# Splitting the stores of the last two heads of an attention backward pass unevenly over the DMA engines

## The chip, the core and the metric

One core of a Trainium2 chip runs the kernel. The metric is device time in microseconds; the median of eight runs of the kernel before is 1289.58 us. The core has five compute engines (TensorE = PE, VectorE = DVE, ScalarE = ACT, GpSimd = POOL, SyncE = SP) and 16 DMA engines that move data between memory and the on-chip buffer of 128 partitions. GpSimd and SyncE issue the DMAs; each has a queue of its own on every DMA engine (in the profile q0 is GpSimd's, "software_dynamic", and q1 SyncE's, "hardware_dynamic").

## The reference

Softmax attention with one query per head, forward and backward, for 2 x 32 = 64 heads, 8192 keys and a head size of 128, all in bfloat16:

```python
def _fwd_reference(q, k, v):
    scale = q.shape[-1] ** -0.5
    scores = jnp.einsum("bhqd,bhkd->bhqk", q, k) * scale
    p = _softmax(scores, axis=-1)
    return jnp.einsum("bhqk,bhkd->bhqd", p, v)

def reference(q, k, v, grad_out):
    out, vjp = jax.vjp(_fwd_reference, q, k, v)
    return (out, *vjp(grad_out))          # out, dq, dk, dv
```

k and v are 2 MB per head, and so are dk and dv. dk of a head is an outer product of a vector over the keys and the query, dv one of the probabilities and grad_out. The kernel reads and writes 268 MB each.

## The kernel before

Heads are numbered 0 to 63. Each head has two tiles, k (w = 0) and v (w = 1), of 128 partitions x 64 keys x 128 values; a partition's row is 16 KB and contiguous in memory. Twelve such tiles fit (`NTILE`), so loads run six heads ahead of the work (`AHEAD`). A tile is loaded (`load`, L98, SyncE), transposed on TensorE (L184), copied by ScalarE (L186), used for scores and for the two accumulations (L195, L339), and at last overwritten in place by `outer` (L394, VectorE) with dk or dv, from where it is stored.

One loop over g, eight steps per head, holds everything in a hand-written order; each instruction is pinned. `outer(i, w, c, ends)` makes quarter c of dv (steps 9 to 12 of a head) or dk (steps 13 to 16), and when c + 1 stands in `ends` it issues the store of what is ready. For all heads but the last `ends` is `whole` = [4], one store of 2 MB per tensor. For the last head it is `last` = [1, 2, 3, 4], one store of 512 KB for each quarter.

Who stores: dk and dv of heads 0 to 62 go by GpSimd (`store_eng`), L412. The last head's eight quarters go by SyncE (`load_eng`), L412 too, then the two small stores of dq and out (L489). dk of the heads 5, 14, ... 59 (`SPREAD`) goes in two pieces, 126 rows and 2 rows, through `by_rows` (L87), which issues one DMA for each number of rows that it is given:

```python
    def by_rows(eng, dst, src, rows):
        p = 0
        for m in rows:
            pin(eng.dma_start(out=dst[p : p + m], in_=src[p : p + m], max_dma_last_dim=NT * D))
            p += m
```

At the start of the kernel the cursor of GpSimd's DMAs is reset (L108, `inc_swdge_sem(..., mode="reset_dge_cursor")`), and GpSimd loads 6 rows of q while SyncE loads the other 58.

A tile's next load waits until the store from it has landed. The framework has eight semaphores for GpSimd's DMAs and eight for SyncE's and uses each in turn: a GpSimd store also waits until the GpSimd store eight before it has landed, and a SyncE DMA until the SyncE DMA eight before it has. At the end of the program SyncE waits for every DMA (L515).

Of the kernel before, what the change touches and what calls it, by code (L numbers as in the profile page):

```python
# [20 lines left out]
SPREAD = range(5, 64, 9)  # L21
# [3 lines left out]
def kernel(  # L25
# [16 lines left out]
    BH = B * H  # L42
# [3 lines left out]
    NCH = NT // CH  # L46
# [3 lines left out]
    load_eng = nc.sync  # L50
    store_eng = nc.gpsimd
    pin = tc.keep_in_program_order
# [30 lines left out]
# [6 lines that stand above are left out]
# [299 lines left out]
    def outer(i, w, c, ends):  # L388

        h = heads[i]  # L390
        n0 = c * CH
        shape = [P, CH, D // 2, 2]
        pin(
            nc.vector.tensor_tensor(  # L394
                out=h.tile[w][:, n0 : n0 + CH, :].rearrange("p n (e t) -> p n e t", t=2),
                in0=h.qb[w][:]
                .rearrange("p (e t) -> p e t", t=2)
                .unsqueeze(1)
                .to_broadcast(shape),
                in1=h.pair[w][:, n0 : n0 + CH, :].unsqueeze(2).to_broadcast(shape),  # L400
                op=ALU.mult,
            )
        )
        if c + 1 in ends:
            at = ends.index(c + 1)
            b0, b1 = (ends[at - 1] if at else 0) * CH, (c + 1) * CH
            dst = (dv_v if w else dk_v)[i]
            if w == 0 and i in SPREAD:
                by_rows(store_eng, dst, h.tile[w], (P - 2, 2))
            else:  # L410
                eng = load_eng if len(ends) > 1 else store_eng
                pin(eng.dma_start(out=dst[:, b0:b1, :], in_=h.tile[w][:, b0:b1, :]))  # L412
# [3 lines left out]
    A0 = A1 + NCH  # L416
    O0 = A0 + 1
    whole = [NCH]
    last = list(range(1, NCH + 1))
    AHEAD = NTILE // 2  # L420

    prev = None
    for g in range(SL * BH + O0 + NCH + 4 - SL):
# [15 lines left out]
        if x := within(O1):  # L439
            outer(x[0], 1, x[1], last if x[0] == BH - 1 else whole)  # L440
        if x := within(O0):
            outer(x[0], 0, x[1], last if x[0] == BH - 1 else whole)
        ev = None
        if g < SL * BH:
            i, r = divmod(g, SL)
# [74 lines left out]
```

## Time and profile before

| | |
|---|---|
| median of 8 runs | 1289.58 us (1285.62 to 1291.8) |
| profiled execution: its own time | 1290.0 us |
| profiled execution: span | 1288.2 us |
| PE / DVE / ACT / POOL busy | 88% / 73% / 76% / 6% |
| HBM read, written | 268.47 MB, 268.47 MB; 417 GB/s over the span |
| last store by GpSimd (dk of head 62) issued | 1245.02 us |
| stores of the last head by SyncE issued | 1247.44 to 1258.1 us |
| small stores of dq and out issued | 1260.86 and 1265.1 us |

The span is the time from the first to the last instruction; the profiled execution's own time is 1.8 us longer. In the profile all times are in us from the start of the span. L12 is line 12 of the kernel. A DMA that a queue issues lands when its last byte is confirmed; between the two lies the time in the queues of the 16 DMA engines. A slice or stretch has a DMA share: the mean share of time in which the 16 engines were busy, so 0.5 can be eight engines at work and eight at rest.

### The profile page before, as it was taken

The numbers are of one execution on the slowest core, as the hardware profiler recorded it, in microseconds if no ns is written. First come the engines' busy times: TensorE is split into PE (matmuls) and PEld (weight loads), VectorE is DVE, ScalarE is ACT, GpSimd is POOL, SyncE is SP. The second block draws the span as 40 slices with busy tenths as digits, with TensorE's granted clock in tenths as the row PEclk, the third lists the DMA queues.
The fourth block names the chain that finished last, engine by engine and source line by source line (L and its number), as shares of the span: only waits on it lengthen the run. The fifth ranks groups of instructions, "written<-read, shape, count | busy, mean of one in ns | idle before, by whom it ended". The sixth has DMA issues, their size and how long they took to land.

```text
span 1288.2 us, 42575 instructions
## 1 busy us (share of the span) xinstructions
PE 1133.8 (88%) x19268; PEld 861.2 (67%) x19268; DVE 936.2 (73%) x2122; ACT 975.7 (76%) x641; POOL 75.3 (6%) x142
## 2 busy tenths in 40 slices
PE   6999999988998988989889898899888988988880
PEld 5777777766676666766667676667666766766650
DVE  2888888777687777767677786778677777777681
ACT  6888888877787777877777787778677777777750
POOL 0000000000000000000000000000000000000000
PEclk9999999999999999989899899999999999999885
DMA  9999999999999999999999999999999999999995
GB/s 387 424 428 428 425 427 428 428 427 427 427 427 426 427 427 427 413 428 427 427 427 426 426 426 427 428 427 424 426 428 428 426 425 423 428 428 427 426 389 208
DMA packets 39986, 539.68 MB, mean 419 GB/s; under 512 B 5116, under 2 KB 5116, under 8 KB 6396
## 3 DMA queue, kind: packets, MB, share of 16 engines
q1 hardware_dynamic: 20172, 272.70, 49.8%
q0 software_dynamic: 19632, 264.25, 48.7%
q8 instruction: 150, 2.46, 0.7%
q14 instruction: 32, 0.26, 0.0%
HBM read 268.47 MB, written 268.47 MB: 417 GB/s over the span
## 4 chain that ended last, share of the span: by engine, by line
DMA 45%; PE 20%; another core or an unknown queue 18%; DVE 10%; issue 3%; ACT 1%; SPq 1%; POOL 0%; DVEq 0%; POOLq 0%; ACTq 0%
DMA kvt<-in_v_dram 24%; DMA kvt<-in_k_dram 17%; PE tp L184 9%; DVE kvt L394 6%; PE acc L339 5%; DMA out_dram<-kvt 3%; PE sw L195 2%; PE dpw L195 2%; DVE sel L362 2%; ACT ev L186 1%; DVE sel L356 1%; SPq L98 1%; PE dpw L282 1%; DMA qd_nat<-in_q_dram 1%
## 5 line engine op out<-in xcount | busy, mean ns | idle before, releaser
L186 ACT COPY ev<-tp 128x2048 bf16<-128x2048 bf16 x512 | 954.9, 1866 | 267.3 <-PE tp L184 256.2
L184 PE MATMUL tp<-ident_bf,kvt 128*128 128x128 bf16 x8192 | 560.9, 223 | 92.2 <-DMA kvt<-in_v_dram 73.8
L394 DVE TENSOR_TENSOR kvt<-qb,pair 128x2048 bf16<-128x2048 bf16 x512 | 621.3, 1214 | 0.4
L184 PEld LDWEIGHTS <-kvt 128*128 128x128 bf16 x8192 | 491.4, 101 | 99.1 <-DMA kvt<-in_v_dram 77.5
L195 PEld LDWEIGHTS <-ev 128*128 128x128 bf16 x8192 | 243.0, 96 | 209.3 <-issue 152.8
L339 PE MATMUL acc<-kvt,dS_pad 128*64 128x512 bf16 x1024 | 169.2, 413 | 0.8 <-DVE dqT L379 0.8
L339 PE MATMUL acc<-kvt,E_pad 128*64 128x512 bf16 x1024 | 161.1, 395 | 0.0
L195 PE MATMUL dpw<-qdT,ev 128*128 128x1 bf16 x4096 | 140.7, 164 | 16.6 <-DVE qb L177 15.8
L362 DVE SCALAR_TENSOR_TENSOR sel<-acc,diag,sel 128x128 f32<-128x128 f32 x384 | 134.7, 351 | 13.6
L195 PE MATMUL sw<-qdT,ev 128*128 128x1 bf16 x4096 | 141.9, 164 | 1.1 <-ACT ev L186 1.1
L412 POOL DMA_DIRECT2D out_dram<-kvt x119 | 64.0, 537 | 1091.6 <-DVE kvt L394 896.4
L207 DVE TENSOR_REDUCE mp<-sw 128x1 f32<-128x64 f32 x64 | 14.4, 225 | 155.6 <-PE sw L195 155.6
L339 PEld LDWEIGHTS <-dS_pad 128*64 128x64 bf16 x1024 | 37.7, 111 | 24.9 <-issue 6.1
L247 DVE CAST E_pad<-E_f 128x64 bf16<-128x64 f32 x64 | 12.5, 195 | 56.4 <-ACT E_f L238 56.4
L339 PEld LDWEIGHTS <-E_pad 128*64 128x64 bf16 x1024 | 36.5, 109 | 21.4 <-issue 0.9
L376 PE MATMUL acc<-ones,sel 128*128 128x1 f32 x256 | 43.5, 239 | 6.2 <-DVE sel L362 6.2
L282 PE MATMUL dpw<-ld,ones 128*128 128x1 f32 x256 | 46.3, 250 | 0.1
L253 DVE CUSTOM_DVE_ANT_0 junk<-E_f,dpw 128x64 bf16<-128x64 f32 x64 | 14.2, 221 | 41.9 <-PE dpw L195 41.9
L376 PEld LDWEIGHTS acc<-ones,sel 128*128 128x128 f32 x256 | 39.3, 194 | 7.3 <-DVE sel L362 7.3
L356 DVE TENSOR_SCALAR sel<-acc,diag 128x128 f32<-128x128 f32 x128 | 44.1, 345 | 0.0
L177 DVE CAST qb<-dpw 128x128 bf16<-128x128 f32 x128 | 35.5, 277 | 6.0 <-PE dpw L168 6.0
L282 PEld LDWEIGHTS dpw<-ld,ones 128*128 128x128 f32 x256 | 38.2, 188 | 0.5 <-DVE ld L253 0.5
(44 smaller groups left out, 313.2 us busy)
## 6 DMA issues: line engine op xcount, KB each, us to landing
out_dram<-kvt POOLq DMA_DIRECT2D x119, 2048.0 KB, 67.2
kvt<-in_v_dram SPq DMA_DIRECT2D x64, 2048.0 KB, 20.7
kvt<-in_k_dram SPq DMA_DIRECT2D x63, 2048.0 KB, 20.7
out_dram<-kvt POOLq DMA_DIRECT2D x7, 2016.0 KB, 70.8
out_dram<-kvt SPq DMA_DIRECT2D x8, 512.0 KB, 24.5
kvt<-in_k_dram SPq DMA_DIRECT2D x2, 512.0 KB, 4.6
kvt<-in_k_dram SPq DMA_DIRECT2D x1, 1024.0 KB, 7.2
out_dram<-kvt POOLq DMA_DIRECT2D x7, 32.0 KB, 70.5
```

The lines of the kernel that those rows point to most:

```text
L177: pin(nc.vector.tensor_copy(out=h.qb[w][:], in_=h.qbp))
L184: pin(nc.tensor.transpose(tp[:, t, :], src[:, c * CH + t, :], ident_bf[:]))
L186: pin(nc.scalar.copy(out=ev[:], in_=tp[:]))
L195: nc.tensor.matmul(dst[:, c * CH + t : c * CH + t + 1], lhsT=ev[:, t, :], rhs=qdT[:, w, i : i + 1], start=True, stop=True,)
L207: pin(nc.vector.reduce_max(out=h.mp[:], in_=h.s, axis=AX.X))
L282: nc.tensor.matmul(out, lhsT=ones[:].to_broadcast([P, P]), rhs=col, start=True, stop=True)
L339: nc.tensor.matmul(h.acc[w][g : g + CW, :], lhsT=wts[:, n0 : n0 + CW], rhs=rows[:, n0 : n0 + QT, :].rearrange("p n d -> p (n d)"), start=( ...
L356: nc.vector.tensor_scalar(out=h.sel[:], in0=block, scalar1=diag[:, 0:1], scalar2=None, op0=ALU.mult)
L362: nc.vector.scalar_tensor_tensor(out=h.sel[:], in0=block, scalar=diag[:, b : b + 1], in1=h.sel[:], op0=ALU.mult, op1=ALU.add,)
L376: nc.tensor.matmul(h.acc[w][:, 0:1], lhsT=h.sel[:], rhs=ones[:], start=True, stop=True)
L394: nc.vector.tensor_tensor(out=h.tile[w][:, n0 : n0 + CH, :].rearrange("p n (e t) -> p n e t", t=2), in0=h.qb[w][:] .rearrange("p (e t) -> ...
L412: pin(eng.dma_start(out=dst[:, b0:b1, :], in_=h.tile[w][:, b0:b1, :]))
```

## The change

The stores of head 62 and the cut of head 63's stores change. dv of head 62 is stored by GpSimd in three pieces of 15, 95 and 18 rows, after a reset of GpSimd's DMA cursor. dk of head 62 goes by SyncE, not GpSimd, in three pieces of 76, 48 and 4 rows. The last head's stores are issued in halves (two for dv, two for dk) where they were issued in quarters. By the author's words the piece of 95 rows lies on DMA engines 15 and 0 to 3.

```diff
@@ outer
             dst = (dv_v if w else dk_v)[i]
-            if w == 0 and i in SPREAD:
+            if i == BH - 2 and w == 1:
+                pin(store_eng.inc_swdge_sem([], [], mode="reset_dge_cursor"))
+                by_rows(store_eng, dst, h.tile[w], (15, 95, 18))
+            elif i == BH - 2:
+                by_rows(load_eng, dst, h.tile[w], (76, 48, 4))
+            elif w == 0 and i in SPREAD:
                 by_rows(store_eng, dst, h.tile[w], (P - 2, 2))
@@ before the loop
     whole = [NCH]
-    last = list(range(1, NCH + 1))
+    last = [NCH // 2, NCH]
     AHEAD = NTILE // 2
```

In the order of the built program nothing else moves. GpSimd's queue ends with the reset and the pieces of 15, 95 and 18 rows in place of two whole stores. SyncE's ends with the pieces of 76, 48 and 4 rows, four halves and the two small stores; the second small store shares its semaphore with the piece of 76 rows and so waits for that piece to land. The changed kernel's lines behind the change are five higher (L412 is L417, L515 is L520).

## The prediction

> **What bounds the kernel now.** I read the page's slices first. They show what is scarce.
>
> ```profile
> DMA  9999999999999999999999999999999999999995
> GB/s 387 424 428 428 425 427 428 428 427 427 427 427 426 427 427 427 413 428 427 427 427 426 426 426 427 428 427 424 426 428 428 426 425 423 428 428 427 426 389 208
> ```
>
> The 16 DMA engines are busy in every slice but the last, at some 427 GB/s. That is 26.7 GB/s an engine, so a row of one head (one partition, 16 KB) costs an engine 0.61 us. The changed stores move the same bytes, so only the last slice (1256 to 1288 us) can give or take anything. Second, the table of stretches of 2 us over the end; the columns that matter are the last two, DMA share and GB/s.
>
> ```profile
> 1258.00:1260.00 2.00, 0.58 (x2) 0.50 (x2) 1.22 (x5) 0.00 (x0) 0.00 (x0) 0.50 1.03 418
> ...
> 1262.00:1264.00 2.00, 0.00 (x0) 0.00 (x0) 0.00 (x0) 0.00 (x0) 0.00 (x0) 0.50 0.67 278
> 1264.00:1266.00 2.00, 0.00 (x0) 0.00 (x0) 0.00 (x0) 0.00 (x0) 0.00 (x0) 0.50 0.57 240
> ...
> 1270.00:1272.00 2.00, 0.00 (x0) 0.00 (x0) 0.00 (x0) 0.00 (x0) 0.00 (x0) 0.50 0.53 222
> ...
> 1278.00:1280.00 2.00, 0.00 (x0) 0.00 (x0) 0.00 (x0) 0.00 (x0) 0.00 (x0) 0.50 0.41 171
> 1280.00:1282.00 2.00, 0.00 (x0) 0.00 (x0) 0.00 (x0) 0.00 (x0) 0.00 (x0) 0.50 0.21 82
> ...
> 1284.00:1286.00 2.00, 0.00 (x0) 0.00 (x0) 0.00 (x0) 0.00 (x0) 0.00 (x0) 0.50 0.12 47
> ```
>
> Times 16, the share counts engines at work: all until 1260, 9 at 1265, 8 at 1271, 7 at 1279, 3 at 1281, 2 at 1285. No compute engine works after 1262. The end is therefore a queue on a few engines while the rest are done. Third, SyncE's waits and the DMA issues say the same from the other side.
>
> ```profile
> SPq L515 <- DMA out_dram<-kvt: 20.5, 4, 17.1
> ```
> ```profile
> out_dram<-kvt POOLq DMA_DIRECT2D x119, 2048.0 KB, 67.2
> kvt<-in_v_dram SPq DMA_DIRECT2D x64, 2048.0 KB, 20.7
> out_dram<-kvt SPq DMA_DIRECT2D x8, 512.0 KB, 24.5
> ```
>
> SyncE's last act is to wait 17.1 us for dk of head 62. A GpSimd store takes 67 us to land, a load 21 us: the wait is in the store queues of the slowest engines.
>
> The packet records have no engine number, but a packet of a busy engine starts 4 ns before its forerunner ends, so I chained them to 16 engines. Their last packets of 4 KB or more end at 1261.4 to 1263.9 (seven engines), 1272.0, 1272.7, 1278.6, 1280.4, 1280.5, 1280.8, 1281.7, 1285.8 and 1286.1, as the shares say. The cause shows too: the 150 instruction packets (16 KB, about 0.98 us) rotate over the same eight engines, 18 or 19 each, some 18 us an engine. Seven of these eight are the seven that end last.
>
> **Which engines get which rows.** In the records the six-row load took six engines, the 58-row load of q by SyncE two engines (29 packets each), a 126-row store fourteen engines (nine rows each) and the two-row piece the other two, the same two in all seven heads. I read this as: the count of engines is the largest number up to 16 that divides the rows, and GpSimd's pieces go round from a cursor. After a reset, then: 15 rows, one each on engines 0 to 14; 95 rows, 19 each on 15 and 0 to 3; 18 rows, two each on 4 to 12. SyncE: 76 rows, 19 each on four engines; 48, three each on all; four, one each on four. No row shows that SyncE's four are 0 to 3; I take it. Of head 62 an engine had 16 rows. It now has 43 (0 to 3), 6 (4 to 12), 4 (13, 14) or 22 (15).
>
> [...]
>
> **Part by part.**
> - Ten rows less on a late engine: 10 x 0.61 = 6.1 us. 1286.0 becomes 1279.9, and the group at 1278.6 to 1281.7 becomes 1272.5 to 1275.6. This lies on the path that sets the end.
> - 27 rows more on engines 0 to 3: 16.5 us. If all four are of the seven early ones, 1262 becomes 1278.5, up to 1280.4 for the latest of the seven. It hides behind the 1279.9 by a hair.
> - Six rows more on engine 15: 3.7 us, 1266 or, if it is one of the two near 1272, 1276. Hidden.
> - The pieces' waits. Each GpSimd store waits for the landing of the GpSimd store eight before it. dv of 62 went at 1234.73: its data was ready at 1234.44, and dk of 58 had landed at 1165.16 + 68.4 = 1233.6. The 15 rows go then too; the 95 rows wait for dv of 59 (issued 1174.24, 64.2 us to land: 1238.4); the 18 rows wait for dk of 59 (1185.36 + 61.8 = 1247.2). Behind them GpSimd has nothing. Engines 0 to 3 must start the 19 rows before they run dry; with 1.1 to 1.6 us from a GpSimd issue to its first packet (the records of dk and dv of 62) that is 1240, and 19 + 23 + 16 rows are then 35 us of work: 1275 plus what is still queued. If the 95 rows came as late as 1247.3, stepping those engines forward row by row gives 1282, a gain of 4 instead of 6.
> - The reset of the cursor: 18 ns at the one place where it stands now (L108). Three issues of 0.58 to 0.80 us (L87's) for one of 0.53: under 2 us of GpSimd, which idles. Nothing, unless the 95 rows are the bound.
> - dk of 62 on SyncE: ready at 1244.7 as now. Three issues stand ahead of dv of 63. The eight stores there cost 0.34 to 1.39 us each, so 4.2 us at most: 1249.2, and the first half of dv of 63 is ready at 1249.4. No cost. If it were 3 us more, the late engines would still have store rows until past 1264.
> - Halves for quarters: per engine 32 packets of 8 KB for 64 of 4 KB, the same 9.8 us. The first two quarters leave 2 us later, the last half at the time of the last quarter (1258.1); on an idle engine it ends 1.2 us later, 1263. Hidden behind 1280 on every engine; 1.2 us if that cover were gone.
> - The second small store of out_0 waits now for the 76 rows' landing: 76 packets of 8 KB in turn on two queues from 1246, 23 us, 1269. The store then needs a few us (the queue makes up its 21.6 now). Hidden by 11 us.
>
> Sum: the last packet goes from 1286.0 to 1279.9 with engines 0 to 3 beside it; from there to the end of the span it was 2.2 us and stays so. The span becomes 1282.2. The profiled execution took 1290.0 with a span of 1288.2, so 1284.0; the median of the eight runs is 1289.58, 0.4 below the profiled one, which I leave inside the range.
>
> **The rivals.**
> - Slower: the heavy share falls on an engine that is not early. It decides from an engine that ended after 1286.0 - 16.5 = 1269.5, and nine of sixteen did. Against it: the relieved pair is 4 and 5 if the cursor stood at 6 after the six-row load, and of this pair one fetches instructions and one does not (it has 511 stretched packets instead, 53 us, and ends at 1272.7). Were the eight fetchers neighbours, they would be 5 to 12, and 0 to 3 early. In my chains the two engines of the 58-row load (0 and 1) end early too, though chains can have swapped. For it: the engine that ends at 1272.0 neither fetches nor is relieved; it is one of 2, 3, 13, 14 and 15, two in five for the heavy ones. Then 1272.0 + 16.5 = 1288.5, the time 1292.5; with a fetching engine among 0 to 3, 1295 to 1302.6, the time 1299 to 1307. [...]
> - Late pieces: the 95 rows held back until 1247 by the semaphore or by room in the queue, 1286 to 1287. For it, GpSimd's stores took up to 74.6 us to land, and 74.6 after 1174.24 is 1248.8; against it, the landing that counts took 64.2 here.
> - The change doesn't do what it says: the pieces spread evenly or over other engines. Late engines save 0 to 4 us: 1286 to 1290.
>
> **How the numbers follow.** About 0.2% (2.6 us) can be told from no change. Forecast 0.52 (1282 to 1286, point 1284.0); late pieces 0.10; spread evenly 0.12, of which most within 0.2%; heavy engine not early 0.26, of which 0.22 slower by over 0.2% and 0.04 within. That makes faster 0.63, same 0.15, slower 0.22. The forecast's own range is 1281.5 to 1286.5; the range reaches into the slower case at its lower price, 1293.5, and leaves out the fetching engine and a little below.
>
> **What would show it.** Right: the share after 1264 stays near 0.7 (0 to 3 and the seven late ones) and falls steeply at 1276 to 1280; dv of 60 to dk of 61 land as before; the GpSimd store of 95 rows is issued near 1238.4, the 18 rows near 1247; SyncE's last wait ends near 1280. Wrong: a share of 0.06 to 0.25 beyond 1283 (one to four engines with the heavy share), or a late issue of the 95 rows, or a late group that ends at 1286 as now.

## The result and the profile after

The changed kernel takes 1302.49 us (median of 11 runs, 1296.14 to 1311.95), the kernel before beside it 1288.52 us (32 runs): ratio 1.0109, interval 1.0093 to 1.0125. It is slower by 1.1%, some 14 us. The prediction of 1284.0 and its range up to 1293.5 both missed. The profiled execution took 1299.66 us, less than the median; its span is 1297.9 us.

The page's slices of the changed kernel first: the share of the DMA engines, and what they moved.

```profile
DMA  9999999999999999999999999999999999999994
GB/s 390 424 427 426 427 427 427 426 428 429 426 427 428 426 427 423 425 427 425 429 428 426 427 428 427 428 424 425 425 428 428 426 426 424 428 427 429 423 315 145
```

Up to slice 38 (1233 us) nothing differs. In slice 39 (1233 to 1265 us) the engines are as busy as ever (a 9), but move 315 GB/s; slice 39 of before, 1224 to 1256 us, had 389. The table of stretches over the same stage says it more sharply; the last two columns are the DMA share and GB/s. The kernel before:

```profile
1236.00:1262.00 26.00, 16.68 (x173) 9.82 (x170) 22.06 (x48) 6.72 (x6) 0.53 (x1) 0.69 0.96 384
1262.00:1280.00 18.00, 0.00 (x0) 0.00 (x0) 0.00 (x0) 0.00 (x0) 0.00 (x0) 0.50 0.52 218
```

The changed kernel:

```profile
1236.00:1262.00 26.00, 14.91 (x142) 8.58 (x137) 20.39 (x43) 5.04 (x5) 1.62 (x2) 0.66 0.94 314
1262.00:1280.00 18.00, 0.00 (x0) 0.00 (x0) 0.00 (x0) 0.00 (x0) 0.00 (x0) 0.50 0.73 245
...
1284.00:1286.00 2.00, 0.00 (x0) 0.00 (x0) 0.00 (x0) 0.00 (x0) 0.00 (x0) 0.50 0.25 103
...
1288.00:1290.00 2.00, 0.00 (x0) 0.00 (x0) 0.00 (x0) 0.00 (x0) 0.00 (x0) 0.50 0.18 72
1290.00:1292.00 2.00, 0.00 (x0) 0.00 (x0) 0.00 (x0) 0.00 (x0) 0.00 (x0) 0.50 0.06 25
```

Divide GB/s by the share and you have what all 16 engines would move if none rested: before 384 / 0.96 = 400 and 218 / 0.52 = 419, after 314 / 0.94 = 334 and 245 / 0.73 = 336. A busy engine moves a sixth to a fifth less. The share alone, which the prediction counted engines by, doesn't show it. In the packet records of 1245 to 1275 us a 16 KB packet takes 732 ns on average (619 before) and one of 8 KB 410 ns (316 in 300 to 1200 us). Most packets keep their time, the medians are 611 and 309 ns; about a quarter take over a tenth longer, these 1.07 us and 0.68 us on average. Summed over all packets behind 1232 us, the time beyond 611, 309 and 159 ns for 16, 8 and 4 KB is 130 us of engine time; before it was 22. I call this sum the stretch. It is one thing that went wrong. The other is at the end of the table: four engines at work at 1285 (0.25 x 16), three at 1289, one from 1290 to 1296.

Which engines these are can be read from the packet records, though they have no engine number: a packet of a busy engine starts some 4 ns before its forerunner ends, so the last ones can be followed back. SyncE's piece of four rows is two packets of 8 KB and one of 4 bytes on each of its four engines alone. The chains that end at 1283.6, 1289.2, 1289.9 (here one record is missing) and 1296.1 us have these packets directly ahead of their 32 packets of halves. So the three engines that end last are three of those with 43 rows.

The issues lie where the prediction had them. GpSimd's timeline, with the idle time before each instruction and its releaser:

```profile
1225.48 0.53 POOL L417 DMA_DIRECT2D out_dram<-kvt  x1 [11.67 <-DVE kvt L394]
1233.13 0.60 POOL L87 DMA_DIRECT2D out_dram<-kvt  x1 [7.12 <-DVE kvt L394]
1236.27 1.03 POOL L87 DMA_DIRECT2D out_dram<-kvt  x1 [2.54 <-DMA out_dram<-kvt]
1243.47 0.59 POOL L87 DMA_DIRECT2D out_dram<-kvt  x1 [6.17 <-DMA out_dram<-kvt]
```

The 95 rows wait 2.54 us and the 18 rows 6.17 us for an older store's landing, and go at 1236.3 and 1243.5 (predicted 1238.4 and 1247.2). SyncE's timeline and its waits:

```profile
1242.97 3.53 SPq L87 DMA_DIRECT2D out_dram<-kvt  x3
1247.67 10.26 SPq L417 DMA_DIRECT2D out_dram<-kvt  x4
1259.09 23.14 SPq L494 DMA_DIRECT2D out_dram<-nat  x2
```
```profile
SPq L494 <- DMA out_dram<-kvt: 14.8, 1, 14.8
SPq L520 <- DMA out_dram<-kvt: 14.1, 4, 5.3
```

The second small store waits 14.8 us for the 76 rows, whose landing was foretold for 1269 and came at 1281.7. The 12.7 us between are the same stretch and queue, seen from one piece. One engine works on to 1296.1 all the same, 14 us longer, so this wait costs nothing itself. The DMA issues, with the size and the time to landing in the last two columns:

```profile
out_dram<-kvt POOLq DMA_DIRECT2D x117, 2048.0 KB, 66.4
out_dram<-kvt SPq DMA_DIRECT2D x4, 1024.0 KB, 40.8
out_dram<-kvt POOLq DMA_DIRECT2D x1, 1520.0 KB, 50.0
```

The whole stores are as before (66.4 us, 67.2 then). The last head's halves land after 40.8 us where the quarters took 24.5 (halves alone, in a run below, 19.0): stores that the change left whole by rows have become late too.

### The profile page after: what moved, and what is told of

It is laid out like the page before. It is cut to its first block, busy times and chain, and to the rows that moved or that the text cites. A ratio compares the mean times of both kernels' runs of the same rounds, so it can differ in the third digit from the quotient of the medians.

```text
span 1297.9 us, 42571 instructions
## 1 busy us (share of the span) xinstructions
PE 1133.9 (87%) x19268; PEld 861.0 (66%) x19268; DVE 936.0 (72%) x2122; ACT 975.7 (75%) x641; POOL 76.5 (6%) x143
## 2 busy tenths in 40 slices
DMA packets 40153, 539.67 MB, mean 416 GB/s; under 512 B 5540, under 2 KB 5540, under 8 KB 5796
## 4 chain that ended last, share of the span: by engine, by line
another core or an unknown queue 34%; DMA 31%; PE 18%; DVE 8%; issue 4%; SPq 1%; ACT 1%; POOL 0%; POOLq 0%; DVEq 0%; ACTq 0%
DMA kvt<-in_v_dram 15%; DMA kvt<-in_k_dram 12%; PE tp L184 8%; PE acc L339 4%; DVE kvt L394 4%; DMA out_dram<-kvt 3%; PE dpw L195 2%; PE sw L195 2%; DVE sel L362 2%; SPq L98 1%; ACT ev L186 1%; DMA qd_nat<-in_q_dram 1%; PE dpw L282 1%; DVE sel L356 1%
## 5 line engine op out<-in xcount | busy, mean ns | idle before, releaser
L417 POOL DMA_DIRECT2D out_dram<-kvt x117 | 62.9, 538 | 1070.5 <-DVE kvt L394 900.4
## 6 DMA issues: line engine op xcount, KB each, us to landing
out_dram<-kvt POOLq DMA_DIRECT2D x117, 2048.0 KB, 66.4
out_dram<-kvt SPq DMA_DIRECT2D x4, 1024.0 KB, 40.8
```

## The experiments

Theory A: a store that is cut by rows stretches the packets while only stores run. Theory B: only the heavy share on an engine that is not early costs. Theory C: the halves cost. Ratios are against the kernel before on the same chip, with a 95% interval. Below, "per full share" is GB/s divided by the DMA share in 1236 to 1262 us (before: 400).

**Only dv of head 62 in pieces** (dk whole, by GpSimd; quarters):

```diff
-            if w == 0 and i in SPREAD:
+            if i == BH - 2 and w == 1:
+                pin(store_eng.inc_swdge_sem([], [], mode="reset_dge_cursor"))
+                by_rows(store_eng, dst, h.tile[w], (15, 95, 18))
+            elif w == 0 and i in SPREAD:
```

> Only dv of head 62 in pieces (15, 95, 18), the rest as before. Theory A (a piece makes an engine read rows outside its usual partitions; with stores alone in flight the engines then hold each other up, and all packets stretch): 1292 to 1298 us, and between 1246 and 1262 fewer GB/s at a full DMA share than the 418 of before (about 340 to 380). Theory B (no stretching, only a heavy share on an engine that is not early): engines 4 to 12 have 5 rows less (3.0 us), the heavy ones 12 more (7.3 us on 1272.0 at most, 1279): 1285 to 1287 us. Theory C (the halves of the last head cost it): 1288.5, as before.

1291.14 us, 1.0034 [1.0024, 1.0044]. Slower, just below A's range and well above B's. Its row of the stage:

```profile
1236.00:1262.00 26.00, 14.08 (x151) 8.39 (x148) 20.64 (x44) 5.28 (x5) 2.20 (x3) 0.70 0.93 326
```

351 per full share; stretch 93 us.

**Only dk of head 62 in pieces by SyncE, with the halves:**

```diff
+            if i == BH - 2 and w == 0:
+                by_rows(load_eng, dst, h.tile[w], (76, 48, 4))
...
-    last = list(range(1, NCH + 1))
+    last = [NCH // 2, NCH]
```

> Only dk of head 62 in pieces (76, 48, 4) by SyncE, and the last head in halves. Theory A: 1292 to 1298 us, GB/s at a full share down as in the kernel with the pieces of dv. Theory B: engines 4 to 15 have 5 rows less (3.0 us), 0 to 3 have 15 more (9.2 us): 1285 to 1287, or 1284 + 2 if the engine near 1272 is among them (1281). Theory C: as the halves alone.

1294.27 us, 1.0052 [1.0033, 1.0071].

```profile
1236.00:1262.00 26.00, 14.84 (x147) 8.47 (x143) 20.52 (x43) 5.16 (x5) 0.00 (x0) 0.67 0.97 346
```

357 per full share; stretch 105 us. Both parts of the change are slower alone. Their sum is 0.86% of the 1.09%; the intervals allow that both together cost nothing more, or up to some 6 us more.

**Only the halves** (`last` alone):

> Only the last head's stores in halves. Theories A and B: no change, 1288 to 1289.5 us. Theory C: most of the 14 us, 1298 or more.

1288.93 us, 1.0015 [1.0000, 1.0029]. 0.15%, at most 0.3%, and a stretch of 26 us: C falls as the cause of the 1.1%.

**dk of head 62 whole, by SyncE, with the halves:**

```diff
-                eng = load_eng if len(ends) > 1 else store_eng
+                eng = load_eng if len(ends) > 1 or (i == BH - 2 and w == 0) else store_eng
...
-    last = list(range(1, NCH + 1))
+    last = [NCH // 2, NCH]
```

> dk of head 62 whole (128 rows) by SyncE in place of GpSimd, and the last head in halves: the queue without the pieces. Theories A and B: within 2 us of before (1287 to 1290.5), and 410 to 420 GB/s between 1248 and 1260. If the queue is what costs it: 1293 or more.

1286.9 us, 0.9993 [0.9982, 1.0005]. It differs from the kernel with pieces by SyncE in 128 rows against (76, 48, 4), and in the packets: a row that goes through `by_rows` is two packets of 8 KB, here it is one of 16.

```profile
1236.00:1262.00 26.00, 14.77 (x158) 8.62 (x154) 21.09 (x45) 5.76 (x5) 0.00 (x0) 0.70 0.94 386
```

411 per full share, stretch 18 us, and the halves land 23.2 us after their issue. So neither SyncE's queue nor a cut by keys (the halves) stretched packets here. Nor did packets of 8 KB by themselves: the halves are 512 of them, with 1.3 us of stretch in all. What is left is the cut by rows. That left two readings, that the cut itself stretches, or that the crowd of rows on a few engines does (theory D).

**Both tensors of head 62 as 64 and 64 rows by GpSimd**, so that by the rule of counts each engine has four rows of each piece, 16 in all as before, and none is heavy:

```diff
-            if w == 0 and i in SPREAD:
+            if i == BH - 2:
+                by_rows(store_eng, dst, h.tile[w], (P // 2, P // 2))
+            elif w == 0 and i in SPREAD:
```

> [...] Theory A (rows out of place in a stage of stores alone stretch packets): 1290 to 1296 us, packets stretched as in the kernel with the pieces of dv. Rival D (the concentration on four or five engines does it): 1286 to 1289, no stretching.

1299.29 us (4 runs), 1.0085 [1.0060, 1.0109].

```profile
1236.00:1262.00 26.00, 14.31 (x136) 8.00 (x133) 20.10 (x43) 4.74 (x5) 1.85 (x3) 0.67 0.98 332
```

339 per full share, stretch 122 us. No engine has a row of head 62 more than before, and most of the loss is there. The crowd is not needed; the cut by rows is enough. (The profiled execution, at 1294.64 us, is the fastest of this kernel's; 122 us can be less than usual.)

**No cut in the last part at all.** The kernel before has one too: dk of head 59 goes as 126 and 2 rows. In its table of stretches the place can be seen, once one looks at both last columns:

```profile
1242.00:1244.00 2.00, 1.80 (x36) 1.09 (x33) 1.49 (x5) 1.70 (x1) 0.00 (x0) 1.00 0.84 307
1244.00:1246.00 2.00, 1.24 (x19) 0.65 (x15) 1.89 (x7) 0.00 (x0) 0.53 (x1) 0.94 0.75 266
1246.00:1248.00 2.00, 1.67 (x8) 1.05 (x10) 1.93 (x5) 0.00 (x0) 0.00 (x0) 0.50 0.95 393
```

307 / 0.84 = 365 and 266 / 0.75 = 355. The two rows ahead of them have 378 and 388, those behind them, up to 1260, 406 to 425.

```diff
-SPREAD = range(5, 64, 9)
+SPREAD = range(5, 55, 9)
```

> dk of head 59 whole, not as 126 and 2 rows; the other six such heads stay. Theory A: the few stretched packets of before (1236 to 1246 us) go and the late engines have one row less, 1 to 4 us faster, 1283 to 1287. Rival D: no stretching to lose, the late engines 0.6 us faster, 1287 to 1288.

1284.34 us, 0.9968 [0.9957, 0.9980]: faster than both kernels. The same two rows:

```profile
1242.00:1244.00 2.00, 2.00 (x41) 1.49 (x39) 1.12 (x2) 1.74 (x4) 0.00 (x0) 1.00 0.73 311
1244.00:1246.00 2.00, 1.80 (x28) 0.94 (x26) 1.86 (x6) 0.97 (x1) 0.00 (x0) 1.00 0.61 254
```

Now 426 and 416 per full share. Stretch behind 1232 us: 5 us, from 22. By rows the edit saves 14 engines one row each (nine become eight), 0.6 us, and 17 us less stretch are 1.1 us an engine on average. It measured 4.1 us; where the rest comes from is open. It isn't an earlier start: dk of head 62 is issued at 1246.29 us, 1.3 later than before.

**Eighteen heads in uneven pieces in mid-run**, meant to give all engines the same end, sized by the prediction's guess that engines 5 to 12 fetch the instructions:

```diff
-SPREAD = range(5, 64, 9)
+SPREAD = {2: (False, (30, 98)), 5: (False, (20, 108)), 8: (True, (24, 104)),
...
+    50: (True, (120, 8)), 53: (True, (18, 110))}
...
```

> dk of 18 heads (2, 5 ... 53) in two pieces whose counts and cursor give the instruction-fetching engines, taken as 5 to 12, about 13 rows less each than the mean before and engines 0 to 3 and 13 to 15 more; all while loads are in flight; no pieces at the end. If theory A holds and the numbers are right: the engines end between 1255 and 1274, 1274 to 1281 us. If the numbers are wrong (the fetchers are others): slower than before, 1292 to 1305. If rows out of place stretch packets beside loads too: no gain, 1288 or more.

1333.38 us, 1.0337 [1.0306, 1.0369]. At the end a share of 0.12 (two engines) lasts past 1320, so the sizes did not give the engines one end. And beside loads too the cut costs, which the page's slices show:

```profile
DMA  9999999999999999999999999999999999999974
GB/s 389 424 426 427 426 427 420 420 414 424 419 423 416 413 401 420 411 423 411 421 405 407 387 423 381 413 391 416 407 395 409 382 424 376 417 411 424 423 315 193
```

Slices with all engines busy fall from 427 to as low as 376 GB/s. The stretch in 300 to 1060 us is 478 us, about 100 in the others.

**The prediction's allocation, far from the end:** without head 59's cut, dv of head 54 as 15, 95 and 18 rows after a reset of the cursor.

> As the kernel with dk of 59 whole, and dv of head 54 in the pieces 15, 95 and 18, which are moved some 150 us before the end, beside loads. Theory A: no stretching there, the late engines 5 rows less: 1 to 3 us faster than the kernel with 59 whole alone, 1281 to 1286. If pieces cost wherever they stand: 4 us slower than it, 1289 to 1292.

1283.74 us, 0.9968 [0.9953, 0.9984], the same as without it. The time is as theory A expected, its reason is not: stretch in 1060 to 1190 us is 47 us (14 to 16 in the kernels with no cut there), so 30 us or more for one tensor, where the pieces at the end cost 93 - 22 = 71. Its records, chained to 16 engines by the prediction's rule of counts and cursor, fit throughout; no view of the profile shows the engines, so what follows rests on these chains. Of the five engines that had the 95 rows one ended at 1263.5, the one without a row of the 15, so engine 15; the others at 1269.7, 1271.4, 1271.9 and 1277.8. Taking off what they had more, one of them, engine 2 or 3, is the one that ended at 1272.0 in the kernel before. The engines that fetch instructions are, by the same chains, not neighbours: they are 13, 14, one of 4 and 5, and five of 6 to 12. A chain can swap engines, so the place of the engine of 1272.0 was put to the test:

**dk of head 62 as 38 and 90 rows by SyncE** in place of 76, 48 and 4: the heavy share (25 rows) falls on the first two engines alone, the third and fourth get six like the rest.

```diff
+            if i == BH - 2 and w == 0:
+                by_rows(load_eng, dst, h.tile[w], (38, 90))
...
-    last = list(range(1, NCH + 1))
+    last = [NCH // 2, NCH]
```

> As the kernel with only dk of 62 in pieces by SyncE and halves, but the pieces are 38 and 90 rows for 76, 48 and 4: 25 rows on the first two engines, 6 on the next thirteen, none on the last. The rows are out of place as much as there. In the run with pieces in head 54 one of the four engines with 95 rows' share ended 6 to 8 us after the other three. If that engine (1272.0 before) is the third or fourth: here it is spared (6 rows for 23, some 10 us), the end is set by the late group with 6 rows for 6 to 16, stretched: 1286 to 1291 us, below the 1294 of the kernel with 76, 48 and 4. If it is the first or second: 25 rows for 23, 1294 or more. If stretching alone counts: as that kernel, 1293 to 1296.

1290.15 us, 1.0020 [1.0011, 1.0029], four us below 76, 48 and 4 with nearly the same stretch (92 against 105 us). The end of the table of stretches, with 76, 48 and 4 rows:

```profile
1284.00:1286.00 2.00, 0.00 (x0) 0.00 (x0) 0.00 (x0) 0.00 (x0) 0.00 (x0) 0.50 0.16 67
1286.00:1288.00 2.00, 0.00 (x0) 0.00 (x0) 0.00 (x0) 0.00 (x0) 0.00 (x0) 0.50 0.11 46
1288.00:1290.00 2.00, 0.00 (x0) 0.00 (x0) 0.00 (x0) 0.00 (x0) 0.00 (x0) 0.50 0.07 29
```

With 38 and 90 rows:

```profile
1284.00:1286.00 2.00, 0.00 (x0) 0.00 (x0) 0.00 (x0) 0.00 (x0) 0.00 (x0) 0.50 0.05 18
1286.00:1288.00 2.00, 0.00 (x0) 0.00 (x0) 0.00 (x0) 0.00 (x0) 0.00 (x0) 0.50 0.00 0
```

The one or two engines that lasted to 1290 are gone. With 76, 48 and 4 rows the two that end last, at 1287.6 and 1290.2, have the two packets of the piece of four rows, so they are heavy ones. That is what the prediction's rival foretold: a heavy engine that was not early. That it is the one of 1272.0 rests on the chains and this one run.

**64 and 64 rows, and 126 and 2, in mid-run** (dv of head 54, without head 59's cut), the even cut by itself beside loads:

> As the kernel with dk of 59 whole (1284.3), and dv of head 54 in two pieces of 64 rows: even shares, out of place, beside loads. If rows out of place stretch packets beside loads too, but less: 20 to 40 us more stretching over the 16 engines there, 1.3 to 2.5 us, 1285.5 to 1287. If beside loads they are free: 1284 to 1285.

1285.67 us, 0.9983 [0.9974, 0.9992], 1.3 us above the kernel without cuts there; stretch 32 us more, 2 us an engine. In 1120 to 1140 us its row, and behind it that of the kernel without the cut:

```profile
1120.00:1140.00 20.00, 18.13 (x307) 13.60 (x308) 15.42 (x35) 16.08 (x11) 1.06 (x2) 1.00 1.00 405
```
```profile
1120.00:1140.00 20.00, 17.10 (x302) 12.97 (x300) 14.56 (x33) 15.03 (x10) 1.06 (x2) 1.00 1.01 430
```

> As the one before, with dv of head 54 in 126 and 2 rows. The six heads stored so before stretch packets by only some 5 us each over the 16 engines: 0.3 us; the late engines have one row more, 0.6: 1284.5 to 1285.5. If any piece costs what the pieces of 64 or of 95 rows cost: as the one before.

1284.3 us, 0.9975 [0.9966, 0.9985], as without it; stretch 14 us more, 0.9 us an engine. This cut costs half as much stretch as 64 and 64 rows, with packets of the same size, and three times the 5 us that had been expected of it. No loss is left in the time; why is open.

**The version to keep:** no cut of head 59, dk of head 62 whole by SyncE, halves.

> The candidate for a version that beats both: dk of 59 whole, dk of 62 whole by SyncE, the last head in halves. The two parts act on different things, so at most the sum of both, 1283 to 1285 us; the second was 0.07% alone, within noise.

1283.68 us, 0.9969 [0.9957, 0.9980]. The same as without head 59's cut alone within noise, so that one line is what helps. Against the changed kernel it is 0.9969 / 1.0109 = 0.986, by way of the kernel before.

## Why the prediction was wrong

**What held.** Where the bound is (a queue on a few engines at the end); the rule of counts, by the small packets that the pieces of dv add (worked out in the last section), and, by the chains of the run with head 54's pieces, that of the cursor; the order and near times of the pieces; the reset takes 18 ns, and dk's move to SyncE costs nothing (0.9993, with the halves); the halves cost 0.15% at the median, with an interval that begins at nothing (predicted nothing); the wait of the second small store is hidden, though it ended 12.7 us later than foretold.

**The step that failed first: "a row of one head costs an engine 0.61 us".** This is a price from whole stores beside loads. It was applied to rows of stores cut by rows, in a stage without loads, and to all other packets of that stage. There 16 KB took 0.73 us on average, and two packets of 8 KB 0.82. The stretch grew by 130 - 22 = 108 us, 6.8 us for each of 16 engines on average. That alone uses up the gain of 6.1 us on the late engines. The run with 64 and 64 rows shows it with no engine heavy: 11 us slower by the medians. The sum had no term for this, and the rival nearest to it ("spread evenly", 1286 to 1290) priced the cut at nothing too. The three heavy engines that do not end last show it too: foretold for 1278.5 to 1280.4, they ended at 1283.6, 1289.2 and 1289.9.

**The step that failed second: "if all four are of the seven early ones".** By the chains, and by the run with 38 and 90 rows, engine 2 or 3 was the one at 1272.0. The rival had this condition and its price: 1272.0 + 16.5 = 1288.5. At the prediction's row price that makes 1292.5 us. The stretch comes on top: this engine has 43 rows of head 62 and 16 of head 63, 59 rows. At 0.12 us more each (16 KB) that is 7.1 us, at 0.20 (two of 8 KB) 11.8. So it ends, by this estimate, between 1295.6 and 1300.3; the last engine, a heavy one, ended at 1296.1. Two in five was a fair chance for the condition by what the trace showed, but the price was short by the stretch, and so the range stopped at 1293.5.

How the 14 us divide can't be read from one sum: the late heavy engine is itself late partly by the stretch. In the profiled execution, 9.7 us slower than that of before, the last packet of data ends at 1296.1 us, and the next engine, heavy too, ends at 1289.9; before, the last packet of data ended at 1286.0. So without the last engine some 3.9 us of the loss would be left, and it adds 6.2. The comparison of (76, 48, 4) with (38, 90) gives about 4 us to its place, where it had fewer rows. The even cut, with no engine heavy, costs 11 us.

**What the profile of before had shown.** The rows at 1242 to 1246 us have 355 to 365 GB/s per full share, in the only stage where a cut store (126 and 2 rows) drained without loads beside it. The prediction counted engines by the share, said that all were at work until 1260, and did not divide. Its first fence has the sign as well: the slice ahead of the last (1224 to 1256 us) is a 9 with 389 GB/s, where the text says that all but the last move some 427. That division was the warning, and removing that cut was the gain.

**Open.** Why a cut by rows stretches other packets as well is not known, whether by the buffer's side or the memory's. A store of 128 rows in packets of 8 KB, or pieces in packets of 16, was not run; the halves speak against the packet size, for SyncE. Theory A, in the expectations, has an engine read rows outside its usual partitions, "out of place"; that was the author's supposition. The packet records name no partition, and no run here varied the partitions at a fixed count, so that is not shown. Also open is why the pieces stretch more at the end (71 us) than beside loads (some 30 us).

## What to carry to other kernels

Divide GB/s by the DMA share before you count engines by the share: here all 16 busy engines moved 334 GB/s with the cut by rows and 400 before. Rows moved between DMA engines by cutting a store by rows were not paid here at the steady price per row: for 0.61 us it was 0.73 on average in one packet of 16 KB and 0.82 in two of 8. Where only stores run, try a store whole first, or cut along its rows' length (the halves of the last head had 1.3 us of stretch in all, its quarters 2.1), and look for cuts that are already there: to take out that of head 59 saved 4.1 us. To load some engines more, know the end of each of them; "seven of sixteen are early" is no address: by the chains one of the four loaded here was the one that had ended at 1272.0.

## What the runs showed of the hardware

- With a cut by rows at the end, the rate per full share falls from 400 GB/s to between 334 and 357. An even cut does so as well (339): both tensors of head 62 as 64 and 64 rows made the kernel 0.85% slower, with as many rows on each engine as before by the rule of counts.
- Pieces bring small packets: the page counts 5540 packets under 512 bytes in the changed kernel and 5116 before, for as many stores; with the pieces of dv alone it is 5596. The 480 more fit a rule: an engine without a row of a GpSimd piece gets a packet of 4 bytes for each data packet of an engine with rows (1 x 2 + 11 x 38 + 7 x 4 = 448), and each store one on all 16 engines (two stores more, 32). SyncE's pieces add none of this kind (5060 against 5052 with the halves alone). They are not the cause of the stretch: 64 and 64 rows have 32 more small packets than before and stretch as much.
- By the chains of packet records the 150 instruction packets fall on eight fixed engines, which are not neighbours, some 18 us on each, and seven of these eight end last before. No view of the profile shows the engines, and no run moved these packets.
